# Infini-attention beside a 2-D Fourier filter on one core: causal zeros spread over three head steps, four copies from ScalarE to VectorE

## The chip, the core and the metric

The kernel runs on one core of a Trainium2 chip. The metric is device time in microseconds (us), here the median of several executions. The engines are TensorE (PE, with its weight loads as PEld), VectorE (DVE), ScalarE (ACT), GpSimd (POOL) and SyncE (SP), which only issues DMAs here. The engines work through their own instruction lists in program order and wait for one another on semaphores.

## What is computed

Two independent results stand side by side in the output. The first is an attention over 2048 positions with 32 heads of 18 columns, in four segments of 512: inside a segment a causal softmax, and beside it a linear memory that earlier segments have filled. A gate per head mixes both. The second is a filter in the frequency domain (a 2-D FFT, a product, the inverse).

```python
for s in range(N):                       # N = 4 segments of 512
    qs, ks, vs = q[:, :, s], k[:, :, s], v[:, :, s]
    logits = einsum("bhqd,bhkd->bhqk", qs, ks) * scale + mask   # causal
    a_dot = einsum("bhqk,bhkd->bhqd", softmax(logits), vs)
    pq = phi(qs)
    num = einsum("bhld,bhde->bhle", pq, M)
    den = einsum("bhld,bhd->bhl", pq, z)[..., None] + 1e-6
    o = g * (num / den) + (1.0 - g) * a_dot
    M = M + einsum("bhld,bhle->bhde", phi(ks), vs)
    z = z + einsum("bhld->bhd", phi(ks))
y = irfft2(rfft2(x) * W)                 # the second result
```

## The kernel before

The order of all instructions is written out by hand: Python generators are advanced one `yield` at a time, and what is emitted first stands first on its engine. The Fourier part and the projections come first, up to about 370 us. Then `attention` runs 133 head steps `t`. One step serves one head of 18 columns in one segment, and four steps make a quad `k` (32 quads: 4 segments of 8).

For each head, three things are done at different steps.

- **Maxima** (`s1`, lines 616 to 640), for the head of step `t+10`, so up to step 117. PE makes logits with queries on the partitions; VectorE takes their row maxima (L627, L633). At step `hh==1` of a quad, `mpath` (L641 to L656) brings the maxima of the quad two later into a bfloat16 pair `mh` on GpSimd (L648, L649); at `hh==3` PE transposes them (L652), ScalarE copies them (`mts`, L655), and GpSimd issues a DMA (L656) that lays them under the queries `Qs`, so that the next logits come out with the maximum subtracted.
- **Exponentials** (`s2`, L658 to L685), for the head of step `t`. PE makes the logits anew with keys on the partitions (L666, L670, L671, L675), ScalarE takes the exponential into three tiles of the quad: `P0` (key block 0 against 512 queries), `P1` (block 1 against 384 queries, then block 3 against 128) and `P2` (block 2 against 256). The first 128 columns of each block hold the diagonal, where the entries above it must become zero. `sel` does that for all four heads of a quad at once: on GpSimd by a selection (L679) in quads 0 to 28, on VectorE by a minimum with a tile `cap` (L680) in quads 29 to 31.
- **Products with the values** (`pv`, L686 to L697): for quad `k` in steps 4k+5 (`jj==0`, reads `P0`), 4k+6 (`jj==1`, reads the first 384 columns of `P1`) and 4k+7 (`jj==2`, reads the last 128 columns of `P1` and then `P2`). `pv_out` copies the sum to SBUF (L701).

In between, the background list `bg` advances at a rate of 1.2 pieces a step: `den`, `mixed`, `oproj`. `mixed(g)` interleaves `combine(g-1)` with `mem1(g,t)`. `combine` takes the attention output of a segment, multiplies it by the reciprocal of the softmax sum (a matmul that spreads the reciprocals over the partitions, L801, and VectorE's product, L806), adds the memory term (L807) and splits the sum into a high part (`oh`, ScalarE, L796) and a low part (`ol`, L797) for the output projection (L822). L797 and L807 are on GpSimd up to step 117, then on VectorE. `mem1` makes the memory term for five groups `t` of heads: a matmul `pn` (L764), a copy to `am` (L766), the spread reciprocals `pb` (L770) and the product (L771). The matmul outputs of all these pieces share one PSUM bank, tag `post`, so each of them waits until the piece before it has been read. `recip` prepares the reciprocals (DVE L720 and L721, ACT L723 and L724, POOL L725 to L727).

`later(k,f)` puts `f` on a list with the due step `now+k`. `due(t)` stands last in a step: it sets `now` to `t` and runs what is due. During step `t`, `now` is therefore still `t-1`.

```python
    def later(s,k,f): s.late.append((s.now+k,f))
    def due(s,now):
        s.now=now; L=s.late; s.late=[]
        for t,f in L:
            if t<=now: f()
            else: s.late.append((t,f))
```

Of the kernel before, what the change touches and what calls it, by code (L numbers as in the profile page):

```python
# [376 lines left out]
class ATT:  # L377
# [280 lines left out]
    def s2(s,t):  # L658
        nc=s.nc; k,hh=divmod(t,4); n,qd=divmod(k,2); h=4*qd+hh
        Q,K=s.Qs[n%3],s.Ks[n%4]; tp=s.tp  # L660
        if hh==0: s.P[k]=[tp.tile([128,4,w],F32,name=f"P{i}") for i,w in enumerate((512,512,256))]
        P=s.P[k]
        q=lambda o: Q[:110,h,o:]
        kk=lambda j: K[:110,h,128*j:128*j+128]
        p0=s.ps.tile([128,512],F32,name="s2",tag="s2")
        nc.tensor.matmul(p0,kk(0),q(0),start=True,stop=True)  # L666
        nc.scalar.activation(P[0][:,hh],p0,AF.Exp,scale=SC)  # L667
        yield
        p1=s.ps.tile([128,512],F32,name="s2",tag="s2")
        nc.tensor.matmul(p1[:,:384],kk(1),q(128),start=True,stop=True)  # L670
        nc.tensor.matmul(p1[:,384:],kk(3),q(384),start=True,stop=True)  # L671
        nc.scalar.activation(P[1][:,hh],p1,AF.Exp,scale=SC)  # L672
        yield
        p2=s.ps.tile([128,256],F32,name="s2",tag="s2")
        nc.tensor.matmul(p2,kk(2),q(256),start=True,stop=True)  # L675
        nc.scalar.activation(P[2][:,hh],p2,AF.Exp,scale=SC)  # L676
        if hh==3:
            def sel(x,pat):
                if k<29: nc.gpsimd.affine_select(out=x,in_=x,pattern=pat+[[1,128]],compare_op=OP.is_ge,fill=0.0,base=0,channel_multiplier=-1)  # L679
                else: nc.vector.tensor_tensor(x,x,s.cap[:,None,:].to_broadcast([128,4,128]),op=OP.min)  # L680
            sel(P[0][:,:,:128],[[0,4]])
            sel(P[1][:,:,:128],[[0,4]])
            sel(P[1][:,:,384:],[[0,4]])
            sel(P[2][:,:,:128],[[0,4]])
        yield  # L685
    def pv(s,k,jj):  # L686

# [73 lines left out]
    def mem1(s,g,t):  # L761
        nc=s.nc; r=126 if t<4 else 72
        pn=s.ps.tile([126,512],F32,name="pn",tag="post")
        nc.tensor.matmul(pn[:r],s.Mst[g][:r,t,:r],s.pq.pop((g,t))[:r],start=True,stop=True)  # L764
        am=s.tp.tile([126,512],F32,name="am",bufs=5)
        nc.scalar.copy(am[:r],pn[:r])  # L766
        if g<3: s.later(1,lambda: s.pq_load(g+1,t))
        yield
        pb=s.ps.tile([126,512],F32,name="pb",tag="post")
        nc.tensor.matmul(pb[:r],s.sel[:,t,:r],s.rc["rd"],start=True,stop=True)  # L770
        nc.vector.tensor_tensor(am[:r],am[:r],pb[:r],op=OP.mult)  # L771
        s.am[t]=am
        yield
# [319 lines left out]
```

## Time and profile before

| | |
|---|---|
| median of three executions | 743.37 us (743.27 to 746.62) |
| profiled execution | 743.75 us, its span 741.7 us |
| granted TensorE clock, mean | 0.993 |
| from the start of the head steps to the end of quad 28's zeros | about 370 to 668 us |
| VectorE minima of quads 29, 30, 31 | 676.15, 688.38 and 698.01 us, 2.49 us each for four |
| copies L766 | 15, 582 to 587 ns each on ScalarE |
| last instructions, output projection of segment 3 | 716 to 742 us |

The profile is one execution, recorded by the hardware. A timeline row has the start, the duration, the engine, the line of the kernel, the operation, output and inputs, and how many instructions were merged; in square brackets stands the idle time of the engine just before, and what ended it. Rows of four merged instructions show the time from the start of the first to the end of the last. On PE, matmuls overlap, so a row's duration is longer than the time until the next may start.

### The profile page before, as it was taken

To read this page: it belongs to the slowest core of one execution; us is meant where nothing else is said; L and a number is where in the kernel's file an instruction comes from. 1 tells how busy PE (TensorE), PEld (TensorE's weight loads), DVE (VectorE), ACT (ScalarE), POOL (GpSimd) and SP (SyncE) were. 2 spreads that over 40 slices of the span, in tenths; PEclk is the share of its full clock that TensorE was granted. 3 is DMA by queue.
4 is the path that set the end of the run, shared out by engine and by line. 5 is a ranking of instruction groups with operands and counts; after the bars stand their busy time and mean duration, and the time that the engine had idled before them with its cause. 6 is when DMAs were issued, how large, how long until landed. Compare 5 with 4: busy or idle time off the path is not lost.

```text
span 741.7 us, 14472 instructions
## 1 busy us (share of the span) xinstructions
PE 696.9 (94%) x5007; PEld 501.1 (68%) x5007; DVE 554.0 (75%) x1288; ACT 457.6 (62%) x1012; POOL 202.8 (27%) x401
## 2 busy tenths in 40 slices
PE   4998999999999999599999999999999999998897
PEld 4988779879789789499944444444565445663397
DVE  5999879899798788288587888887566875655533
ACT  3666796585694674144387777777566775656631
POOL 2111000100200114256155334545143762333010
PEclk9999999999999999899999999999999999999999
DMA  9884435555473368879637665777546765431052
GB/s 332 264 269 142 143 123 174 192 173 157 149 238 108 120 206 250 216 197 211 187 115 177 170 166 142 182 168 162 141 102 176 180 165 134 101 101 41 24 156 75
DMA packets 83245, 121.05 MB, mean 163 GB/s; under 512 B 11353, under 2 KB 50631, under 8 KB 83037
## 3 DMA queue, kind: packets, MB, share of 16 engines
q1 hardware_dynamic: 76580, 104.11, 49.5%
q0 software_dynamic: 6592, 16.03, 8.0%
q8 instruction: 39, 0.64, 0.4%
q14 instruction: 34, 0.27, 0.1%
HBM read 81.78 MB, written 38.24 MB: 162 GB/s over the span
## 4 chain that ended last, share of the span: by engine, by line
PE 72%; DMA 5%; DVE 4%; ACT 3%; issue 1%; POOL 1%; SPq 0%; DVEq 0%; ACTq 0%
PE pj L451 12%; PE pv L695 10%; PE s L623 9%; PE pjv L451 8%; PE po L822 6%; PE i L296 4%; PE i L307 4%; PE s L666 3%; PE s L670 3%; PE po L851 2%; PE pn L764 2%; DMA Ks<-qkD 2%; PE s L675 2%; PE s L632 2%; PE pm L508 2%
## 5 line engine op out<-in xcount | busy, mean ns | idle before, releaser
L627 DVE CUSTOM_DVE_ANT_0 junk<-s,mask 128x512 bf16<-128x512 f32 (+1 forms) x256 | 141.3, 552 | 61.1 <-PE s L623 57.6
L623 PE MATMUL s<-Ks,Qs 108*128 108x384 bf16 (+3 forms) x512 | 138.2, 302 | 9.9 <-DMA Ks<-qkD 7.3
L633 DVE TENSOR_REDUCE mx<-s 128x4 f32<-128x512 f32 x128 | 87.9, 687 | 20.2 <-PE s L632 18.4
L623 PEld LDWEIGHTS <-Qs 108*128 108x128 bf16 x512 | 50.6, 99 | 59.8 <-issue 44.4
L695 PE MATMUL pv<-P,vs 128*32 128x512 f32 (+3 forms) x1024 | 89.1, 442 | 1.1 <-ACT am L766 1.1
L679 POOL TENSOR_SCALAR_AFFINE_SELECT P<-P 128x512 f32<-128x512 f32 x116 | 70.1, 634 | 69.2 <-ACT P L667 61.4
L667 ACT ACTIVATE P<-s 128x512 f32<-128x512 f32 x128 | 76.4, 597 | 13.6 <-PE s L666 10.9
L676 ACT ACTIVATE P<-s 128x256 f32<-128x256 f32 x128 | 49.2, 385 | 51.3 <-PE s L675 50.8
L672 ACT ACTIVATE P<-s 128x512 f32<-128x512 f32 x128 | 76.2, 595 | 0.0
L451 PE MATMUL pj<-xh,wqkl 128*128 128x512 f32 x180 | 71.1, 395 | 0.0
L451 PE MATMUL pj<-xh,wqkh 128*128 128x512 f32 x180 | 71.1, 395 | 0.0
L451 PE MATMUL pj<-xl,wqkh 128*128 128x512 f32 x144 | 61.8, 429 | 0.0
L666 PE MATMUL s<-Qs,Ks 110*128 110x512 bf16 x128 | 48.8, 381 | 2.2 <-DMA Qs<-mts 1.4
L206 DVE TENSOR_TENSOR Z<-t,t 128x290 f32<-128x290 f32 (+1 forms) x96 | 48.4, 555 | 0.1
L451 PE MATMUL pjv<-wvh,xh 128*128 128x288 f32 x160 | 48.1, 303 | 0.0
L451 PE MATMUL pjv<-wvl,xh 128*128 128x288 f32 x160 | 46.2, 295 | 0.0
L206 DVE TENSOR_TENSOR t<-Z 128x580 f32<-128x580 f32 x64 | 46.1, 756 | 0.0
L498 POOL MEMSET vt<- 128x32 f32 x16 | 2.3, 161 | 150.4 <-PE pm L508 128.8
L632 PE MATMUL s<-tri,idb 128*128 128x128 bf16 x256 | 43.2, 220 | 0.0
L296 PE MATMUL i<-civ,Y 128*128 128x256 f32 (+1 forms) x288 | 40.2, 293 | 1.9 <-DVE t L206 1.7
L670 PE MATMUL s<-Qs,Ks 110*128 110x384 bf16 x128 | 41.9, 327 | 0.1
L142 PE MATMUL f<-ftab,eh 128*128 128x290 f32 (+1 forms) x160 | 30.7, 309 | 10.4 <-DMA ftab<-ftab 10.4
(169 smaller groups left out, 1628.6 us busy)
## 6 DMA issues: line engine op xcount, KB each, us to landing
qkD<-sp SPq DMA_DIRECT2D x36, 384.0 KB
Qs<-qkD SPq DMA_DIRECT2D x96, 144.0 KB
Ks<-qkD SPq DMA_DIRECT2D x96, 144.0 KB
xin<-xb SPq DMA_DIRECT2D x16, 384.0 KB
cfw<-cfw POOLq DMA_DIRECT2D x16, 384.0 KB, 4.5
civ<-civ POOLq DMA_DIRECT2D x16, 384.0 KB, 8.3
vs<-vD SPq DMA_DIRECT2D x16, 330.0 KB
vD<-vt SPq DMA_DIRECT2D x16, 311.0 KB
```

Source lines behind the costliest of these rows:

```text
L206: v.tensor_tensor(o,a,b,op=op)
L296: nc.tensor.matmul(p[:m,k],Y[i][:,q,c*128:c*128+m],cc[:,hl,o:o+256],start=n==0,stop=n==5)
L451: s.nc.tensor.matmul(out,a,b,start=i==0,stop=i==len(L)-1)
L623: nc.tensor.matmul(out,Q[:108,h,128*i:128*i+128],K[:108,h,:128*(i+1)],start=True,stop=True)
L627: nc.vector.tensor_tensor_reduce(out=junk[:,:w],in0=src,in1=s.mask[:,512-w:],scale=1.0,scalar=-3.0e38, op0=OP.add,op1=OP.max,accum_out=s.m ...
L633: nc.vector.tensor_reduce(out=s.mx[k][:,hh],in_=pa.rearrange("p (b c) -> p b c",c=128),axis=mybir.AxisListType.X,op=OP.max)
L666: nc.tensor.matmul(p0,kk(0),q(0),start=True,stop=True)
L667: nc.scalar.activation(P[0][:,hh],p0,AF.Exp,scale=SC)
L670: nc.tensor.matmul(p1[:,:384],kk(1),q(128),start=True,stop=True)
L672: nc.scalar.activation(P[1][:,hh],p1,AF.Exp,scale=SC)
L679: if k<29: nc.gpsimd.affine_select(out=x,in_=x,pattern=pat+[[1,128]],compare_op=OP.is_ge,fill=0.0,base=0,channel_multiplier=-1)
L695: nc.tensor.matmul(s.pvt[32*hh:32*hh+32,128*j:],vt[:,j,19*h:19*h+32],mv[0][:,hh,mv[1]],start=j==0,stop=j==2,skip_group_check=True)
```

## The change

The four selections of a quad are no longer emitted together in the last step of the quad. The one on `P0` stays. The one on the first 128 columns of `P1` is emitted at the end of the next step, those on `P2` and on the last 128 columns of `P1` at the end of the step after that, the one on `P2` first. This holds for GpSimd's selections and for VectorE's minima alike. The pattern of the selection, always the same, moves into `sel`.

The copy in `mem1` is emitted on VectorE instead of ScalarE when `now` is 119 or more: the last four of segment 3's five copies.

```diff
         if hh==3:
-            def sel(x,pat):
-                if k<29: nc.gpsimd.affine_select(out=x,in_=x,pattern=pat+[[1,128]],compare_op=OP.is_ge,fill=0.0,base=0,channel_multiplier=-1)
+            def sel(x):
+                if k<29: nc.gpsimd.affine_select(out=x,in_=x,pattern=[[0,4],[1,128]],compare_op=OP.is_ge,fill=0.0,base=0,channel_multiplier=-1)
                 else: nc.vector.tensor_tensor(x,x,s.cap[:,None,:].to_broadcast([128,4,128]),op=OP.min)
-            sel(P[0][:,:,:128],[[0,4]])
-            sel(P[1][:,:,:128],[[0,4]])
-            sel(P[1][:,:,384:],[[0,4]])
-            sel(P[2][:,:,:128],[[0,4]])
+            sel(P[0][:,:,:128])
+            s.later(2,lambda: sel(P[1][:,:,:128]))
+            s.later(3,lambda: sel(P[2][:,:,:128]))
+            s.later(3,lambda: sel(P[1][:,:,384:]))
```

```diff
         am=s.tp.tile([126,512],F32,name="am",bufs=5)
-        nc.scalar.copy(am[:r],pn[:r])
+        (nc.vector.tensor_copy if s.now>=119 else nc.scalar.copy)(am[:r],pn[:r])
```

## The prediction

> **What bounds the kernel now.** I read the page first, then the busy time by windows, the waits of PE, and the timelines of POOL, DVE, ACT and PE at every place where PE stood.
>
> ```profile
> span 741.7 us, 14472 instructions
> PE 696.9 (94%) x5007; PEld 501.1 (68%) x5007; DVE 554.0 (75%) x1288; ACT 457.6 (62%) x1012; POOL 202.8 (27%) x401
> ```
>
> ```profile
> 380.00:676.00 296.00, 290.14 (x2407) 152.09 (x2406) 214.30 (x630) 205.69 (x492) 132.92 (x240) 1.00 0.59 148
> ```
>
> (The last row is a window: its length, then the busy time of PE, PEld, DVE, ACT and POOL, the granted clock, the DMA share and GB/s.) TensorE bounds it. In the stage that the change touches first (quads 0 to 28, 380 to 676 us) PE is busy for 290.1 of 296.0 us, POOL for 132.9. The zeros are POOL's work there and hidden, as long as no PV matmul waits for them. So the first edit can only give back some of 5.9 us of PE's idle time, or take cover away. From quad 29 on (676 to about 704 us) the zeros are on DVE and PE has real holes; there the order on DVE and ACT counts.
>
> Each quad k has its exponentials in steps 4k to 4k+3 and its PV in three later steps: PV0 (reads P0) in 4k+5, PV1 (P1, first 384 columns) in 4k+6, PV2 (P1's last 128 columns first, then P2) in 4k+7.
>
> **The change part by part.**
>
> *Part 1, the zeros on POOL (quads 0 to 28).* No instruction is added or removed; `sel(P1[:128])` goes to the end of step 4k+4, P2 and P1's last columns to the end of 4k+5. `later(2)` and `later(3)` count from the step before, since `due` sets `now` last. The order of POOL becomes: P0, the DMA of the maxima (L656), first selection of P1, the two `mh` operations (L648, L649), P2, last selection of P1. What is queued in a step ahead of `due` (the pieces of `combine`, L797 and L807, and `recip`, L725 to L727) now stands ahead of zeros that used to be long done. On SP's queue nothing moves. PV1 waits for P1's first selection alone, PV2 for the last one.
>
> ```profile
> L679 POOL TENSOR_SCALAR_AFFINE_SELECT P<-P 128x512 f32<-128x512 f32 x116 | 70.1, 634 | 69.2 <-ACT P L667 61.4
> ```
>
> One selection takes 0.63 us; four in a row take 2.39 us (rows below), so they follow each other every 0.59 us. What it gives:
>
> ```profile
> 395.41 2.39 POOL L679 TENSOR_SCALAR_AFFINE_SELECT P<-P 128x512 f32<-128x512 f32 x4
> 397.75 0.61 POOL L656 DMA_DIRECT2D Qs<-mts  x1
> ```
>
> ```profile
> 394.42 0.24 ACT L655 COPY mts<-mt 32x128 bf16<-32x128 bf16 x1
> ```
>
> ```profile
> 404.13 0.39 PE L666 MATMUL s<-Qs,Ks 110*128 110x512 bf16 x1 [1.44 <-DMA Qs<-mts]
> ```
>
> The largest PE wait before 676 us: a logits matmul of quad 4 waits 1.44 us for the maxima's DMA, issued behind four selections at 397.75 though `mts` was ready at 394.66. Behind one selection it starts at about 396.0, 1.75 us earlier, more than the wait: **−1.44**, if the landing moves with the issue. Ahead of it one small loss eats into it:
>
> ```profile
> 391.37 0.22 POOL L649 TENSOR_TENSOR mh<-mg,mh 128x16 bf16<-128x16 f32 x1
> ```
>
> ```profile
> 392.66 0.86 PE L695 MATMUL pv<-P,vs 128*32 128x128 f32 x16
> ```
>
> Quad 1: the second `mh` lets POOL go at 391.55; P2 and the last P1 selection (0.59+0.63) end at 392.77, with a hand-over of some 0.05 us against PV2 at 392.66: +0.17. Net **−1.27**.
>
> What it costs elsewhere is read from the same sum, end of `mh` plus 1.22 us, against PV2. The first and the last of the usual quads:
>
> ```profile
> 382.29 0.22 POOL L649 TENSOR_TENSOR mh<-mg,mh 128x16 bf16<-128x16 f32 x1
> ...
> 663.59 0.22 POOL L649 TENSOR_TENSOR mh<-mg,mh 128x16 bf16<-128x16 f32 x1
> ```
>
> ```profile
> 384.42 0.86 PE L695 MATMUL pv<-P,vs 128*32 128x128 f32 x16
> ...
> 665.72 0.86 PE L695 MATMUL pv<-P,vs 128*32 128x128 f32 x16
> ```
>
> `mh` lets POOL go 0.17 us after its start, 382.46 and 663.76; 1.22 more gives 383.68 and 664.98, both 0.74 us ahead of PV2. Of the 29 quads taken in this way from the two timelines, 14 have 0.5 to 0.75 us to spare, 12 have more, quad 1 has none, and in two more `combine` puts operations in between:
>
> ```profile
> 581.19 0.22 POOL L649 TENSOR_TENSOR mh<-mg,mh 128x16 bf16<-128x16 f32 x1
> 581.36 1.27 POOL L797 TENSOR_TENSOR ol<-am,oh 126x512 fp32r<-126x512 f32 x1
> 582.60 1.27 POOL L807 TENSOR_TENSOR am<-ux,am 126x512 f32<-126x512 f32 x1
> ```
>
> ```profile
> 584.03 0.86 PE L695 MATMUL pv<-P,vs 128*32 128x128 f32 x16
> ```
>
> Quad 20: L797 and L807 were queued before `due`, so P2 starts at 583.84 and the last selection ends at 585.06. PV2 goes at 585.12 instead of 584.03: **+1.09**. Right behind it DVE waits for PE, too, so there is no backlog that would absorb the delay:
>
> ```profile
> 585.29 0.69 DVE L771 TENSOR_TENSOR am<-am,pb 126x512 f32<-126x512 f32 x1 [0.51 <-PE pb L770]
> ```
>
> Quad 28 has the same order:
>
> ```profile
> 669.03 2.52 POOL L807 TENSOR_TENSOR am<-ux,am 126x512 f32<-126x512 f32 x2
> 671.50 1.27 POOL L797 TENSOR_TENSOR ol<-am,oh 126x512 fp32r<-126x512 f32 x1
> 672.74 1.25 POOL L807 TENSOR_TENSOR am<-ux,am 126x512 f32<-126x512 f32 x1
> 674.21 0.22 POOL L649 TENSOR_TENSOR mh<-mg,mh 128x16 bf16<-128x16 f32 x1
> ```
>
> ```profile
> 669.23 0.68 DVE L806 TENSOR_TENSOR ux<-ux,pb 126x512 f32<-126x512 f32 x1
> ```
>
> ```profile
> 674.29 0.86 PE L695 MATMUL pv<-P,vs 128*32 128x128 f32 x16
> ```
>
> Quad 28: the second L807 needs the `ux` that DVE ends at 669.91, so it ends at about 671.2; P1's first selection makes 671.8; L797, L807 and both `mh` (674.21+0.17−671.50 = 2.88 us in the rows) make 674.65; P2 and the last selection 675.87. PV2 goes at 675.93: **+1.64**. Behind it on PE stand the `pb` of L770, L652 and the logits of step 120, and ACT's exponentials wait for these.
>
> *Part 2, the zeros of quads 29 to 31 and the four copies (L766) on DVE.* They move as before, P0 in step 4k+3; each copy leaves ACT's queue and enters DVE's. The largest hole:
>
> ```profile
> 676.15 2.49 DVE L680 TENSOR_TENSOR P<-P,cap 128x512 f32<-128x512 f32 x4
> 678.56 0.69 DVE L797 TENSOR_TENSOR ol<-am,oh 126x512 fp32r<-126x512 f32 x1
> 679.16 0.68 DVE L806 TENSOR_TENSOR ux<-ux,pb 126x512 f32<-126x512 f32 x1
> ```
>
> ```profile
> 677.79 0.60 ACT L796 CAST oh<-am 126x512 fp32r<-126x512 f32 x1
> ```
>
> ```profile
> 679.89 2.07 PE L764 MATMUL pn<-pq,Mst 126*126 126x512 f32 x2 [3.12 <-DVE ux L806]
> ```
>
> PE waits 3.12 us for `ux`, and four selections stand before it. With one, DVE would be free at 676.76; but L797 comes first and needs `oh`, which a closed row of ACT work delivers at 678.39. So the hole shrinks by **0.15** only; ACT is next in line. The copies cannot help, the first one moved comes behind this place.
>
> ```profile
> 688.95 0.59 ACT L766 COPY am<-pn 126x512 f32<-126x512 f32 x1 [1.27 <-PE pn L764]
> 689.43 0.39 ACT L676 ACTIVATE P<-s 128x256 f32<-128x256 f32 x1
> ```
>
> ```profile
> 690.86 0.38 PE L666 MATMUL s<-Qs,Ks 110*128 110x512 bf16 x1 [0.71 <-ACT P L667]
> ```
>
> The copy holds ACT for 0.48 us, ACT goes on without a gap until 690.8, and PE waits for it. Off ACT, the exponentials and PE come 0.4 us earlier. On DVE, idle there, the copy costs nothing that PE sees. Its price isn't shown: below, the 288-column copy (0.46, next row); above, 0.68 us for L771, which also reads PSUM over 512 columns. I take 0.60 to 0.69.
>
> ```profile
> L993 DVE COPY P<-po 128x288 f32<-128x288 f32 x4 | 1.8, 459 | 5.5 <-PE po L851 5.5
> ```
>
> ```profile
> 698.01 2.49 DVE L680 TENSOR_TENSOR P<-P,cap 128x512 f32<-128x512 f32 x4
> 700.42 0.94 DVE L721 RECIPROCAL ry<-ry 128x128 f32<-128x128 f32 x1
> 701.28 0.62 DVE L771 TENSOR_TENSOR am<-am,pb 72x512 f32<-72x512 f32 x1
> ```
>
> ```profile
> 701.96 0.93 PE L822 MATMUL po<-woh,oh 126*128 126x288 f32 x5 [0.94 <-DVE am L771]
> ```
>
> The end of the stage: L771 now stands behind P0, a copy, the reciprocal and one selection (0.60+0.60+0.86+0.60) instead of four selections and the reciprocal, and the row starts 0.45 earlier. L771 starts at 700.2 (697.56 and 2.66); PV1 (needs that selection) ends at 701.1, and the projection L822 starts there: **−0.85** in all for the copies and the order, the 0.4 included. From there to the end PE and the DMAs follow one another, so it stays.
>
> **Sum:** −1.27 +1.09 +1.64 −0.15 −0.85 = **+0.46 us**. The profiled execution took 743.75 us (span 741.7), 0.38 above the median of the runs, 743.37. Against the median: 743.8, say **743.9 us**.
>
> Bounds of the terms: DMA wait −1.44 to 0; quad 20 from +0.5 to +1.2 and quad 28 from 0 (if the pieces of `combine` come earlier) to +1.8; the tail −1.6 (both selections behind L771 and the copy gone from its way) to 0.
>
> **The clock** is one more term.
>
> ```profile
> 679.86:683.27 3.41, 3.38 (x9) 1.15 (x13) 0.69 (x1) 1.27 (x3) 0.00 (x0) 0.50 0.02 5
> ```
>
> This window's granted clock is 0.50: after the 3.12 us hole PE runs at half speed for 3.41 us, busy all the time, and 1.7 us are lost. The hole stays in my forecast (about 3.0 us, behind a new one of 1.6), so I keep the loss. The Trainium skill (TensorE: Matmul & The Clock Gate, What's actually happening) says that the clock halves after an idle window of about 3.4 us and that the windows run freely. [...] The trace agrees on the 3.41 us of the slow stretch, not on the whole idle window: the hole had 3.12 us. The first rival below is what this rule would do here.
>
> **Rivals.**
> - *The hole falls otherwise and the clock holds:* 1.7 us less, 742.2. For it: the hole gets shorter and starts at another moment. Against: it shrinks by 5% only. 0.20.
> - *The DMA doesn't land earlier:* the engines are 59% busy over the stage; if others hold the transfer, 1.27 comes back: 745.2. The row of all 32 speaks for it a little, the latencies lie far apart. 0.12.
>
> ```profile
> DMA to landing us min/median/max: 2.0/5.0/8.4
> ```
>
> The Trainium skill (DMA: Bandwidth & Descriptors, Anatomy of one DMA) gives 2.0 us plus bytes over 436e3 for such a DMA; an estimate from it, 2.02 us for 8 KB, would land at 399.8 and leave no wait to remove. Only the fastest one here agrees.
> - *Slower: PV2 waits in every usual quad.* The place is the last selection of P1 behind both `mh`. The point is the 0.74 us of the usual quad: if POOL is later by 1.0 us there (a `mh` that waits longer, a slower hand-over), 14 quads lose about 0.3 each, 4.2 us: 748.1. Against: the selections are all alike and `mh` keeps its place. 0.11.
> - *Faster, the change does what it seems meant to:* the two POOL waits don't show, DMA wait and copies pay in full, the clock holds: −1.44−0.15−0.85−1.7: 739.2. Against: the queued L797 and L807. 0.07.
>
> **How the numbers follow.** My forecast has 0.50. 0.5% is 3.7 us, about what a measurement of this kernel can tell from no change: within it lie the forecast, the first and the second rival, 0.82; slower 0.11, faster 0.07. The range leaves these two out and takes in 742.2 and 745.2 with the unknown terms, some 1.2 us on either side: 741.2 to 746.4; the forecast alone has 742.7 to 745.1.
>
> **What would show it.** The DMA wait at 404 us gone; new waits of PE for L679 near 584 (1.1 us) and 674 us (1.6 us), none in the usual quads; the hole before L764 still near 3 us, now behind `oh` of ACT; L766 on DVE 0.60 to 0.69 us; from quad 28's PV2 to the start of L822 26.7 us instead of 27.7 (701.96−674.29, less 0.15 and 0.85). Wrong if PE waits for L679 in many quads, if that hole closes, or if the clock column differs.

## The result and the profile after

The changed kernel takes 748.3 us (median of 21 executions, 745.4 to 756.5). The kernel before, executed beside it, takes 744.5 us (21 executions, 741.7 to 748.4). The ratio on record is 1.0062 (that of the two medians is 1.0052), with a 95% interval of 1.0043 to 1.0082: slower by 3.2 to 6.1 us, where the prediction had +0.5 us. The profiled execution took 747.5 us, near the median, against 743.75 us before. (The profile of experiment e5 below was of a disturbed execution and is not read.)

The page of the changed kernel, first the span and the busy times, then two groups (duration of all, mean of one in ns, idle time in front):

```profile
span 745.5 us, 14461 instructions
...
PE 698.6 (94%) x5007; PEld 504.0 (68%) x5007; DVE 556.1 (75%) x1292; ACT 455.5 (61%) x1008; POOL 204.9 (27%) x401
...
L695 PE MATMUL pv<-P,vs 128*32 128x512 f32 (+3 forms) x1024 | 89.7, 445 | 4.3 <-POOL P L679 2.6
...
L679 POOL TENSOR_SCALAR_AFFINE_SELECT P<-P 128x512 f32<-128x512 f32 x116 | 72.6, 639 | 35.7 <-ACT P L667 35.5
```

PE has hardly more to do, and of the 4.3 us that it waits ahead of value products (L695) 2.6 us are now due to the selections. The timeline of PE shows the places:

```profile
583.25 0.86 PE L695 MATMUL pv<-P,vs 128*32 128x128 f32 x16 [1.00 <-POOL P L679]
...
675.22 0.86 PE L695 MATMUL pv<-P,vs 128*32 128x128 f32 x16 [1.64 <-POOL P L679]
...
680.70 1.12 PE L764 MATMUL pn<-pq,Mst 126*126 126x512 f32 x2 [2.99 <-DVE ux L806]
...
710.13 0.38 PE L831 MATMUL pb<-rr,sel 96*126 96x512 bf16 x1
...
715.13 0.38 PE L831 MATMUL pb<-rr,sel 96*126 96x512 bf16 x1 [2.63 <-DVE ux L832]
```

The first three rows are what the prediction asked for: 1.0 us near 584, 1.6 us near 674, a hole of 3.0 us before L764; and the DMA wait at 404 us is gone. The fifth is not in it. L831 is the matmul that spreads the reciprocals for the last segment's five tiles. The second of them waits 2.63 us for PSUM that VectorE's product L832 has to read. The window after it (length, PE, PEld, DVE, ACT, POOL busy, granted clock, DMA share, GB/s) stands at half clock:

```profile
715.94:719.35 3.41, 3.41 (x16) 3.41 (x15) 2.61 (x4) 2.43 (x6) 0.00 (x0) 0.50 0.17 38
```

The same place in the kernel before, in the timelines of PE, SP, POOL and VectorE:

```profile
702.22 0.42 POOL L725 TENSOR_TENSOR ry<-ry,rw 128x128 f32<-128x128 f32 x1 [24.87 <-ACT rw L724]
```

```profile
705.43 0.32 SPq L733 DMA_DIRECT2D rr<-rrD  x1
...
708.93 1.34 SPq L784 DMA_DIRECT2D ux<-uD  x3
```

```profile
710.11 0.38 PE L831 MATMUL pb<-rr,sel 96*126 96x512 bf16 x1
...
712.89 0.38 PE L831 MATMUL pb<-rr,sel 96*126 96x512 bf16 x1 [0.41 <-DVE ux L832]
```

```profile
712.15 0.69 DVE L832 TENSOR_TENSOR ux<-ux,pb 126x512 f32<-126x512 f32 x1 [10.24 <-DMA ux<-uD]
```

And in the kernel after:

```profile
701.45 1.78 POOL L725 TENSOR_TENSOR ry<-ry,rw 128x128 f32<-128x128 f32 x1 [23.18 <-ACT rw L724]
```

```profile
701.66 1.28 DVE L680 TENSOR_TENSOR P<-P,cap 128x512 f32<-128x512 f32 x2
714.38 0.69 DVE L832 TENSOR_TENSOR ux<-ux,pb 126x512 f32<-126x512 f32 x1 [11.45 <-DMA ux<-uD]
```

```profile
706.29 0.32 SPq L733 DMA_DIRECT2D rr<-rrD  x1
...
709.70 1.28 SPq L784 DMA_DIRECT2D ux<-uD  x3
```

L725 belongs to the `recip` that makes the reciprocals `rr`; they go through memory, and L733 loads them. `ux` is the attention output, loaded back from memory (L784) for the product L832. Read from quad 28's PV2 on, which takes out what happened earlier (674.29 before, 675.22 after):

| from PV2 of quad 28, us | before | after | shift |
|---|---|---|---|
| projection L822 starts | 27.67 | 26.76 | −0.91 |
| L725 of POOL starts | 27.93 | 26.23 | −1.70 |
| L725 ends | 28.35 | 28.01 | −0.34 |
| ux loads issued (L784) | 34.64 | 34.48 | −0.16 |
| first L831 | 35.82 | 34.91 | −0.91 |
| first ux load used (L832) | 37.86 | 39.16 | +1.30 |
| second L831 | 38.60 | 39.91 | +1.31 |

PE arrives 0.91 us earlier; the prediction had 1.00 (0.15 and 0.85). The loads that it then needs are not earlier: the reciprocal started 1.70 us sooner, but its POOL operation L725, now beside two minima of quad 31 on VectorE, takes 1.78 us instead of 0.42, and SP issues the ux loads behind that chain in program order. The loads also take longer to land (39.16−34.48 = 4.68 us instead of 3.22). The hole grows by 0.91−0.16+1.46 = 2.21 us (2.63−0.41 = 2.22 in the rows), and half a clock over 3.41 us follows, an estimated 1.7 us at most. The third L831 stands 44.58 us behind PV2 instead of 41.74, so 2.84 of the 3.8 us that the span grew are lost here. Of the rest, 1.19 us came before the first PV2 (385.61 instead of 384.42 us), where PE waits for nothing that was changed, and −0.26 between the two PV2.

### The profile page after: what moved, and what is told of

It reads as the page before. It is cut to its first block, busy times and chain, and to the rows that moved or that the text cites. A ratio compares the mean times of both kernels' runs of the same rounds, so it can differ in the third digit from the quotient of the medians.

```text
span 745.5 us, 14461 instructions
## 1 busy us (share of the span) xinstructions
PE 698.6 (94%) x5007; PEld 504.0 (68%) x5007; DVE 556.1 (75%) x1292; ACT 455.5 (61%) x1008; POOL 204.9 (27%) x401
## 4 chain that ended last, share of the span: by engine, by line
PE 70%; DMA 6%; issue 4%; DVE 3%; ACT 2%; POOL 2%; SPq 1%; DVEq 0%; ACTq 0%; POOLq 0%
PE pj L451 11%; PE s L623 10%; PE pv L695 9%; PE pjv L451 8%; PE po L822 6%; PE i L307 4%; PE i L296 4%; PE s L666 3%; PE s L670 2%; PE po L851 2%; PE s L675 2%; PE s L632 2%; DMA Ks<-qkD 2%; PE pm L508 2%; PE pn L764 1%
## 5 line engine op out<-in xcount | busy, mean ns | idle before, releaser
L623 PE MATMUL s<-Ks,Qs 108*128 108x384 bf16 (+3 forms) x512 | 138.5, 303 | 11.7 <-DMA Ks<-qkD 9.8
L695 PE MATMUL pv<-P,vs 128*32 128x512 f32 (+3 forms) x1024 | 89.7, 445 | 4.3 <-POOL P L679 2.6
L623 PEld LDWEIGHTS <-Qs 108*128 108x128 bf16 x512 | 50.7, 99 | 61.3 <-issue 44.9
L679 POOL TENSOR_SCALAR_AFFINE_SELECT P<-P 128x512 f32<-128x512 f32 x116 | 72.6, 639 | 35.7 <-ACT P L667 35.5
```

The source lines that it names most:

```text
L623: nc.tensor.matmul(out,Q[:108,h,128*i:128*i+128],K[:108,h,:128*(i+1)],start=True,stop=True)
L679: if k<29: nc.gpsimd.affine_select(out=x,in_=x,pattern=[[0,4],[1,128]],compare_op=OP.is_ge,fill=0.0,base=0,channel_multiplier=-1)
L695: nc.tensor.matmul(s.pvt[32*hh:32*hh+32,128*j:],vt[:,j,19*h:19*h+32],mv[0][:,hh,mv[1]],start=j==0,stop=j==2,skip_group_check=True)
```

## Experiments

Theory T1: the loss beyond the prediction is this chain. Rivals: T2, the two waits of PV2 for POOL with what they set off; T3, chance in where PE's idle time falls; T4, the copies on VectorE. Each ratio is to the kernel before, executed on the same chip, with its 95% interval. Line numbers are those of the profile; edits keep them.

**e1, the copies alone.**

```diff
-        nc.scalar.copy(am[:r],pn[:r])
+        (nc.vector.tensor_copy if s.now>=119 else nc.scalar.copy)(am[:r],pn[:r])
```

> The kernel before with the four last copies of L766 on VectorE and nothing else. Theory T1 (the loss of the whole change sits after 704 us: the selections of quad 31 that now stand behind the reciprocal run beside L725 of POOL, SP's queue is held, the ux loads come late, and the hole before L831 halves the clock): the four selections still end ahead of the reciprocal, so L725 stays at 0.4 us, the hole before L831 stays at 0.4 us or below, and the time is 0 to 0.5 us less, ratio 0.999 to 1.000. Rival T4 (the copies on VectorE cost what was lost): ratio 1.004 to 1.006. Rival T3 (the loss is where the idle windows of PE fall by chance): any ratio of 0.997 to 1.003, with the granted clock as the only difference.

Measured: 1.0015 (0.999 to 1.0041), above the 0.999 to 1.000 that T1 expected. L725 takes 0.42 us and the hole before L831 0.61, as T1 says. But the last copy stands behind four minima on VectorE, and PE waits for it; the timeline of PE and the windows:

```profile
698.35 1.06 PE L695 MATMUL pv<-P,vs 128*32 128x512 f32 x8 [1.06 <-DVE P L680]
700.67 0.38 PE L770 MATMUL pb<-rd,sel 96*72 96x512 bf16 x1 [1.25 <-DVE am L766]
```

```profile
697.69:701.10 3.41, 1.50 (x13) 0.43 (x17) 3.41 (x6) 0.00 (x0) 0.00 (x0) 1.00 0.00 0
701.10:704.51 3.41, 3.41 (x17) 2.19 (x14) 0.92 (x2) 0.70 (x2) 1.14 (x3) 0.50 0.02 5
```

Two short holes fall into one stretch of 3.41 us, PE is busy for 1.50 us of it, and the next stretch runs at half clock. The copies are free only while the minima are dealt out. T4 as a cause of the whole loss falls.

**e2, the zeros on POOL alone.**

```diff
-            sel(P[0][:,:,:128])
-            s.later(2,lambda: sel(P[1][:,:,:128]))
+            df=s.later if k<29 else lambda i,f: f(); sel(P[0][:,:,:128])
+            df(2,lambda: sel(P[1][:,:,:128]))
...
```

> Only the zeros of POOL (quads 0 to 28) are dealt over three steps; those of VectorE stay together and the copies stay on ScalarE. T1: the waits for L679 near 584 (1.1 us) and 674 us (1.6 us) show, the DMA wait at 404 us is gone, L725 stays at 0.4 us, the hole before L831 near 0.4 us: +1.5 us in all, ratio 1.001 to 1.003. Rival T2 (the two waits of PV2 for POOL are what the whole change lost, by what they set off behind them): ratio 1.004 to 1.007.

Measured: 1.0037 (1.0015 to 1.0058), that is 1.1 to 4.3 us. Both waits are there, L725 takes 0.42 us, and the hole before L831 is small:

```profile
583.90 0.86 PE L695 MATMUL pv<-P,vs 128*32 128x128 f32 x16 [0.99 <-POOL P L679]
...
675.86 0.86 PE L695 MATMUL pv<-P,vs 128*32 128x128 f32 x16 [1.63 <-POOL P L679]
...
714.91 0.38 PE L831 MATMUL pb<-rr,sel 96*126 96x512 bf16 x1 [0.80 <-DVE ux L832]
```

Between the two theories: a good part of the loss, about half, sits here. It was in the prediction, as +1.46 us, and the interval holds that.

**e3, the zeros on VectorE alone** (`df=s.later if k>=29`, the copies on ScalarE).

> Only the zeros of VectorE (quads 29 to 31) are dealt over three steps; those of POOL stay together and the copies stay on ScalarE. T1: L725 of POOL runs beside two selections of quad 31 and takes over 1.2 us instead of 0.42, L733 and the ux loads are issued 0.6 to 0.9 us later, the hole before L831 is 2 us or more and half clock follows it: ratio 1.003 to 1.005. T2: nothing of the loss is here, ratio 0.998 to 1.000. T3: as T2, or the clock alone.

Measured: 1.0023 (0.9996 to 1.005), below the 1.003 to 1.005 that T1 expected, with an interval that holds both theories; the times alone do not decide. The profile does for the place of the hole, though the copies and POOL's selections are those of before:

```profile
700.18 2.04 POOL L725 TENSOR_TENSOR ry<-ry,rw 128x128 f32<-128x128 f32 x1 [22.93 <-ACT rw L724]
```

```profile
714.02 0.38 PE L831 MATMUL pb<-rr,sel 96*126 96x512 bf16 x1 [2.73 <-DVE ux L832]
```

**e4, the whole change with the loads early.** They read rows that earlier heads wrote.

```diff
             if t==125: lane.append(s.recip(s.rD[3],s.rrD[3],s.g1,False,"rr"))
+            if t==130: [s.ux_load(3,u) for u in range(3)]
...
-        for u in range(3): s.ux_load(3,u)
```

> The whole change, and the three first ux loads of the last group are issued at the start of step 130, ahead of L733 and of the transfers of U in SP's queue, instead of behind them. Their rows were written by earlier heads. T1: the loads land before 710 us, the hole before L831 (2.63 us in the profile of the changed kernel, 0.41 in that of before) and the half clock behind it go, though L725 is as slow as before: 3 to 4.5 us less than the changed kernel, ratio to the kernel before 0.999 to 1.002. T2 and T3: the ratio stays at 1.005 to 1.007.

Measured: 0.9989 (0.9961 to 1.0017). L725 is as slow as ever, but the loads no longer hang on it, and VectorE's product waits for PE instead of a DMA:

```profile
699.31 1.77 POOL L725 TENSOR_TENSOR ry<-ry,rw 128x128 f32<-128x128 f32 x1 [23.26 <-ACT rw L724]
```

```profile
708.61 0.69 DVE L832 TENSOR_TENSOR ux<-ux,pb 126x512 f32<-126x512 f32 x1 [7.82 <-PE pb L831]
```

PE has no wait of 0.4 us or more at L831, and no half clock there. The loss of the change is gone with an edit that touches none of its instructions.

**e5, the kernel before with the loads early** (the same edit).

> The kernel before with the three first ux loads of the last group at the start of step 130, as in e4. Theory T1 (the changed kernel loses its time because PE gets to the projection earlier while the chain reciprocal, SP's queue, ux loads is not earlier, and a hole and half clock follow): here the hole before L831 is only 0.4 to 0.8 us, so the early loads bring 0.4 to 0.8 us, ratio 0.999 to 1.000. Rival: the early loads are worth 4 us to any kernel (they also clear the DMA queue for what follows), ratio 0.994 to 0.996, and e4 then says nothing of what the change lost.

Measured: 0.9978 (0.9948 to 1.0008). More than expected, 1.6 us, with an interval that holds the expected 0.4 to 0.8 (the medians, 743.75 and 744.32 us, differ by 0.6). In the changed kernel the same edit is worth some 4.5 to 5.4 us (from 1.0050 in e11 or 1.0062 to 0.9989). About 3 to 4 us of what e4 gains are thus the change's own loss there, with some 2 us of uncertainty on each of the two.

**e6, quad 31's minima together again** (`df=s.later if k<31`, the rest as in the change).

> The whole change except for quad 31, whose four selections stay together in step 127, ahead of the reciprocal. T1: L725 of POOL is back at 0.42 us, the hole before L831 at 0.4 to 0.9 us without half clock behind it; the two waits for L679 (1.0 and 1.6 us) stay: ratio 1.001 to 1.003, 2 to 4 us less than the whole change. Rival T2 (the waits of PV2 for POOL and what they set off are the loss): ratio stays at 1.005 to 1.007.

Measured: 1.0029 (0.9998 to 1.0059). As T1 says, at the place in question:

```profile
703.14 0.42 POOL L725 TENSOR_TENSOR ry<-ry,rw 128x128 f32<-128x128 f32 x1 [24.90 <-ACT rw L724]
```

```profile
716.63 0.38 PE L831 MATMUL pb<-rr,sel 96*126 96x512 bf16 x1 [0.84 <-DVE ux L832]
```

But the half clock came elsewhere, as in e1, where PE waits for the last copy:

```profile
701.48 0.59 PE L770 MATMUL pb<-rd,sel 96*72 96x512 bf16 x1 [1.25 <-DVE am L766]
```

```profile
700.82:707.65 6.83, 6.17 (x32) 4.12 (x35) 2.01 (x4) 0.91 (x3) 1.14 (x3) 0.50 0.08 17
```

So e6 tells the cause of the hole, not its price.

**e7, the delay without the change.** The kernel before, with idle copies ahead of L725.

```diff
+        [nc.gpsimd.tensor_copy(w[:,2],y) for _ in range(4 if dst is s.rrD[3] else 0)]; nc.gpsimd.tensor_tensor(y,y,w[:,0],op=OP.subtract)
```

> The kernel before with four idle copies of 128x128 on POOL ahead of L725 in the recip of step 125 (about 1.4 us, what L725 was slowed by in the changed kernel); nothing else is touched and no selection is moved. T1: L729, L733 and the ux loads come 1.4 us later, the hole before L831 grows from 0.4 to 1.8 us (3 us if the loads also take 4.5 us instead of 3.3 to land); with half clock behind it the time is 3 to 4.5 us more, without it 1.4: ratio 1.002 to 1.006. Rival T3 (POOL's chain has slack there, the late loads were the DMA queue of that run): ratio 0.999 to 1.001.

Measured: 1.005 (1.0019 to 1.008), as large a loss as the whole change's, out of 1.4 us on a POOL that is otherwise idle:

```profile
700.44 1.36 POOL L725 CAST rw<-ry 128x128 bf16<-128x128 f32 x4 [25.52 <-ACT ry L723]
701.89 0.42 POOL L725 TENSOR_TENSOR ry<-ry,rw 128x128 f32<-128x128 f32 x1
```

```profile
713.74 0.58 PE L831 MATMUL pb<-rr,sel 96*126 96x512 bf16 x1 [2.69 <-DVE ux L832]
```

```profile
713.78:717.19 3.41, 3.41 (x14) 3.33 (x14) 3.38 (x5) 1.84 (x4) 0.00 (x0) 0.50 0.03 10
```

T3 falls: POOL's chain has no slack there, and its delay alone brings the hole and the half clock.

**e8, POOL's zeros in two steps** (with e4's loads).

```diff
-            s.later(3,lambda: sel(P[2][:,:,:128]))
-            s.later(3,lambda: sel(P[1][:,:,384:]))
+            s.later(c,lambda: sel(P[2][:,:,:128]))
+            s.later(c,lambda: sel(P[1][:,:,384:]))
```

Here `c` is 2 for quads 0 to 28 and 3 for the others.

> e4 (the whole change with the early ux loads), and on POOL (quads 0 to 28) both zeros of P1 and that of P2 are issued at the end of step 4k+4, so that they stand ahead of the mh operations and of the pieces of combine of step 4k+5. The waits of PE for L679 near 584 (1.0 us) and 674 us (1.6 us) go, the DMA of the maxima still stands behind one selection only: 2 to 3 us less than e4, ratio to the kernel before 0.995 to 0.997. If the waits are made up for later anyway (PE catches up on ACT or DMA), as e4: 0.998 to 1.000.

Measured: 0.9977 (0.9946 to 1.0008). No wait for L679 is left; a shorter one stands in its place (0.48 us, PE's transpose for `mh` of POOL at 675.5), and the profiled execution waits 1.87 us for a load of `Ks` at 486. The gain on e4, 0.9 us, is below the 2 to 3 expected and smaller than either interval.

**e9, a store held back** (the whole change; the first `ya` of segment 2's projection stands behind the ux loads on SP).

```diff
-                if hf==1: s.later(1,lambda tb=tb,ob=ob: ...
+                if hf==1: s.later(2 if g==2 and tb==0 else 1,lambda tb=tb,ob=ob: ...
```

> The whole change, with one store of the group before (ya of its first 128 rows, 288 KB) issued behind the three ux loads and the last transfer of U in SP's queue instead of between two transfers of U. If that store, which stands ahead of the ux loads in the DMA queues, is what makes them take 4.7 us instead of 3.2 to land: landing 3.2 us or less, hole before L831 1.0 us instead of 2.6, half clock gone there, 2 to 3 us less than the changed kernel, ratio 1.001 to 1.004. If the landing does not depend on it: hole 2.2 to 2.7 us, ratio 1.005 to 1.007.

Measured: 1.0003 (0.9975 to 1.0031), but the profiled execution is one of the longest of its twelve (749.6 us, their median is 745.6) and shows a landing of 4.92 us (711.55 to 716.47) and a hole of 2.09 us:

```profile
717.21 0.38 PE L831 MATMUL pb<-rr,sel 96*126 96x512 bf16 x1 [2.09 <-DVE ux L832]
```

The times speak for the store as a cause of the long landing, the profile against it. Inconclusive.

**e10, the recip operations on VectorE** (the whole change).

```diff
+        eg=nc.vector if dst is s.rrD[3] else nc.gpsimd; eg.tensor_tensor(y,y,w[:,0],op=OP.subtract)
+        eg.tensor_copy(w[:,1],y)
+        eg.tensor_tensor(w[:,2],y,w[:,1],op=OP.subtract)
```

> The whole change, with the three operations of the recip of step 125 (L725 to L727) on VectorE, where they stand ahead of the last two selections of quad 31, instead of on POOL beside them. Theory T1 (L725 was slowed by the selections that run beside it): the chain ends about 1.4 us earlier, L733 and the ux loads with it, hole before L831 1.2 us or less and no half clock behind it: 2.5 to 4 us less than the changed kernel, ratio 1.000 to 1.003. Rival (the three operations were not the late link; the landing of the loads or SP's queue is): hole 2 us or more, ratio 1.005 to 1.007.

Measured: 1.0004 (0.9981 to 1.0026). The order of the minima is that of the change, the meeting of the two engines is taken away (and L725 is shorter on VectorE, 0.28 us instead of 0.42):

```profile
701.33 0.28 DVE L725 TENSOR_TENSOR ry<-ry,rw 128x128 f32<-128x128 f32 x1
...
702.12 1.29 DVE L680 TENSOR_TENSOR P<-P,cap 128x512 f32<-128x512 f32 x2
```

```profile
712.63 0.38 PE L831 MATMUL pb<-rr,sel 96*126 96x512 bf16 x1 [0.45 <-DVE ux L832]
```

**e11, the change once more.**

> The whole change once more, unaltered, beside the others of this group: ratio 1.005 to 1.007, hole before L831 2.4 to 2.8 us with half clock behind it, waits for L679 of 1.0 and 1.6 us. Where the profile differs from the first one (the wait for Ks near 305 us, the start of the first PV2), it is what changes from one execution to the next. If chance decides (T3), the hole before L831 differs by 1 us or more.

Measured: 1.005 (1.0023 to 1.0077). The two waits are there again (0.99 and 1.63 us), L725 takes 1.77 us, half clock runs from 716.60 to 720.01 us, and

```profile
715.50 0.38 PE L831 MATMUL pb<-rr,sel 96*126 96x512 bf16 x1 [2.76 <-DVE ux L832]
```

What varies is PE's wait at about 310 us, ahead of L623 (7.28 us before and 9.80 in the first profile after, both for `Ks`; 7.82 here, where the profile shows no releaser); the first PV2 comes at 383.86 us here. The 1.19 us of the first profile were chance.

**e12, the low parts last** (e8, and from step 117 on L797 on VectorE behind the products).

```diff
-                eng().tensor_tensor(s.ol[u][:r],x[:r],s.oh[u][:r].bitcast(F32),op=OP.subtract)
+                low=lambda o=s.ol[u][:r],x=x[:r],h=s.oh[u][:r].bitcast(F32): eng().tensor_tensor(o,x,h,op=OP.subtract)
...
-                r=126 if t<4 else 72; x=xs[t]
+                r=126 if t<4 else 72; x=xs[t]; t>1 and s.now<117 and low()
...
-                    eng().tensor_tensor(s.am[t][:r],x[:r],s.am[t][:r],op=OP.add)
+                    eng().tensor_tensor(s.am[t][:r],x[:r],s.am[t][:r],op=OP.add); t>1 and s.now>=117 and low()
...
-            yield
+            t>4 and low(); yield
```

> e8 (zeros of POOL in two steps, copies and zeros of VectorE as in the whole change, early ux loads), and in combine from step 117 on the difference L797 is issued on VectorE behind the products of the same tile (L806, L807) instead of ahead of them, since it waits for oh of ScalarE. VectorE is free at about 676.8 us for L806, so the hole of 3.1 us before L764 falls to 1 us or less and the half clock behind it (1.7 us) goes: 3 to 4.5 us less than e8, ratio to the kernel before 0.992 to 0.995. If oh or the pb of PE is the next limit at once: hole stays over 2.5 us, ratio 0.997 to 0.999.

Measured: 0.9889 (0.9856 to 0.9922), 736.8 us, the fastest of all and faster than both kernels. The timelines of VectorE and PE:

```profile
675.47 0.69 DVE L680 TENSOR_TENSOR P<-P,cap 128x512 f32<-128x512 f32 x1
676.43 0.69 DVE L806 TENSOR_TENSOR ux<-ux,pb 126x512 f32<-126x512 f32 x1 [0.28 <-PE pb L801]
677.15 0.69 DVE L807 TENSOR_TENSOR am<-ux,am 126x512 f32<-126x512 f32 x1
678.28 0.69 DVE L797 TENSOR_TENSOR ol<-am,oh 126x512 fp32r<-126x512 f32 x1 [0.44 <-ACT oh L796]
```

```profile
677.17 1.12 PE L764 MATMUL pn<-pq,Mst 126*126 126x512 f32 x2 [0.67 <-DVE ux L806]
```

The hole before L764 falls to 0.67 us (3.12 in e8, 2.99 in the change), and the half clock behind it is gone.

**e13, the ry load behind the ux loads** (the whole change; L716 after L784 on SP).

```diff
-        b=s.recip(s.rD[3],s.rrD[0],s.g1,False,"rd"); next(b)
-        for u in range(3): s.ux_load(3,u)
+        b=s.recip(s.rD[3],s.rrD[0],s.g1,False,"rd")
+        for u in range(3): s.ux_load(3,u); next(b) if u==2 else None
```

> The whole change, with the ry load of the last group (L716, which waits on SP for rD and reads rows of 512 bytes) issued behind the three ux loads instead of ahead of them. The ux loads are issued 0.5 to 0.9 us earlier by that alone. If the ry load is what makes them land late: 3.2 us or less from issue to landing, hole before L831 under 0.6 us, no half clock, ratio 1.000 to 1.003. If not: 4.4 us or more from issue to landing, hole 1.7 to 2.2 us, ratio 1.003 to 1.006.

Measured: 1.0036 (1.0009 to 1.0062). The loads still take 4.64 us (709.80 to 714.44); the `ry` load is not what holds them. The hole of 1.76 us brings no half clock:

```profile
715.18 0.38 PE L831 MATMUL pb<-rr,sel 96*126 96x512 bf16 x1 [1.76 <-DVE ux L832]
```

```profile
713.41:716.82 3.41, 1.65 (x13) 1.61 (x12) 2.31 (x4) 0.92 (x2) 0.00 (x0) 1.00 0.42 144
716.82:720.23 3.41, 3.41 (x27) 3.38 (x26) 3.28 (x6) 1.97 (x6) 0.74 (x1) 1.00 0.34 90
```

**e14, e12 without the change:** the kernel before with the edits of e4 and e12.

> e12 without any of the change: the kernel before, with the early ux loads and with L797 behind the products. If the zeros dealt out on VectorE are what lets L806 go early, the four selections still stand before it here, the hole before L764 is 2.4 us or more with half clock behind it: ratio 0.994 to 0.998, 4 us or more above e12. If the order of L797 alone closes the hole: as e12, 0.987 to 0.991.

Measured: 0.9944 (0.9921 to 0.9967). Four minima stand before L806, and the hole before L764 is back:

```profile
679.52 2.02 PE L764 MATMUL pn<-pq,Mst 126*126 126x512 f32 x2 [2.52 <-DVE ux L806]
```

Against e12 this is some 4 us, with about 3 us of uncertainty either way. e14 leaves out the whole change, POOL's part too: in the two profiles 1.9 us of the difference lie between the first PV2 and quad 28's, where chance moves about as much, and 3.5 us behind it (62.4 us to the end of the span in e12, 65.9 here). So with L797 out of the way and the loads early, the dealt minima and the copies on VectorE are worth about 3.5 us in this pair; in the change as it was made, neither was so.

## Why the prediction was wrong

It was wrong in one step, which it put in one sentence: "From there to the end PE and the DMAs follow one another, so it stays." The other terms came out close to what was worked out, the first with some luck:

| term | predicted, us | shown |
|---|---|---|
| DMA wait at 404 us goes | −1.44 | gone in every profile with dealt zeros on POOL; in those without, 1.44, 0.51, 0.54 and 1.05, and none at that place in e3: the forecast took the largest of five |
| quad 1's PV2 comes late | +0.17 | 2.27 us behind PV1 instead of 2.11: +0.16 |
| quad 20's PV2 waits for L679 | +1.09 | wait 1.00, PV2 4.13 us behind PV1 instead of 3.06: +1.07 |
| quad 28's PV2 waits for L679 | +1.64 | wait 1.64 |
| hole before L764 shrinks | −0.15 | 3.12 to 2.99 |
| copies and order up to L822 | −0.85, with the −0.15 PV2 to L822 26.7 | 26.76, shift −0.91 |
| copy on VectorE | 0.60 to 0.69 us each | 0.68 to 0.69 |
| from there to the end | 0 | third L831 at +2.84 instead of −1.00 (−0.15 and −0.85): 3.8 us |

*POOL's part.* Over the stretch from the first quad's PV2 to quad 28's, the five profiles with the selections together (before, e1, e3, e7, e14) have 287.6 to 290.0 us, mean 289.1; the eight with three steps (after, e2, e4, e6, e9, e10, e11, e13) have 289.6 to 291.9, mean 290.8. The difference, 1.7 us, stands beside −1.27+1.09+1.64 = 1.46; single pairs scatter (before and after alone give −0.26). With the 2.84 us of the end it makes 4.5 us, inside the measured 3.2 to 6.1. The two with two steps (e8, e12) have 289.3 and 288.1. No usual quad waits: the slower rival did not occur, and the second one neither (the DMA did land earlier). The wait that the forecast calls the largest before 676 us is so only from 380 us on; at 310 us PE waits 7.28.

*The end.* What it missed has two halves. The −0.15 and −0.85 move PE alone. PE then meets loads which hang on another chain (reciprocal, ScalarE, POOL's L725 to L727, a round trip through memory, SP's list) and were already late by 0.41 us before. And that chain could not move with PE, because the same dealing put two minima beside L725. The prediction named L725 to L727 only among what stands ahead of selections on POOL; beside VectorE's zeros it gave them no price. It also said that on SP's queue nothing moves, which holds for the order and misses what the order does: the ux loads, which need nothing of this chain, stand behind it. e10 takes away the meeting, e4 the hanging together, e7 puts the delay alone into the kernel before; all three came out as T1 expected, e4 at the edge of its range. e4 and e10 keep both waits of PV2 for POOL, so T2 does not explain the rest of the loss.

The Trainium skill (SBUF — State Buffer, SBUF: two separate sides) says that a GpSimd operation and a VectorE operation with two inputs in SBUF exclude each other through one pair of ports, whole instruction by whole instruction. L725 beside the minima, 1.78 us instead of 0.42, agrees: it ends 0.29 us after the second minimum. The kernel before already shows this price, in the last `recip`, where L833 has both inputs in SBUF:

```profile
717.17 0.69 DVE L833 TENSOR_TENSOR ux<-ux,am 126x512 f32<-126x512 f32 x1
```

```profile
717.20 0.95 POOL L725 TENSOR_TENSOR ry<-ry,rw 128x128 f32<-128x128 f32 x1 [13.70 <-ACT rw L724]
```

L725 starts 0.03 us behind L833, takes 0.95 us and again ends 0.29 us after it. That such a meeting has a price could have been read from these rows before the prediction. That whichever starts first keeps the ports is seen in e4: L725 starts at 714.55 and takes 0.43 us, and L833, from 714.70, takes 0.82 instead of 0.69. It is not seen beside the minima, where L725's record starts 0.21 us ahead of them, in e3 0.47 us, and L725 waits all the same; why stays open.

*The clock.* The prediction kept one half clock, behind the hole before L764. It is there (681.81 to 685.22). A second one comes behind the new hole. Rival one, that the clock holds, did not occur.

*Open.* Of the hole's 2.2 us, 1.46 are the longer landing of the ux loads (4.4 to 4.9 us in the profiles of after, e3, e7, e9, e11 and e13; 2.9 to 3.6 in those of before, e1, e2, e6 and e10; in e2 and e6 at most, since L832 waits for PE there). The `ry` load is not its cause (e13); e9 does not settle the store; other causes were not tried. The longer landing came with the delay alone in e7 (4.51 us). It is not more data: in the 6 us from the issue of the loads the queues move 1.15 MB before and 1.14 after, but in the first 3 us the DMA engines are 85% busy before and 66% after.

## What to carry to other kernels

When an edit brings PE earlier to a place, follow each operand it reads next back to its own chain, and ask of every engine on that chain what the same edit has put beside it; a gain that reaches one operand only becomes a hole. Look in an in-order DMA queue for loads that wait behind a chain they don't need: issuing three of them earlier was worth 4.5 to 5.4 us in the changed kernel, about as much as the change had lost, and some 1.6 us or less without the change. And a change that pays nothing may be waiting for the next obstacle: the dealt minima and the copies were worth about 3.5 us in one pair of profiles once L797 no longer stood in front of L806 and the loads came early.

## What the hardware showed beside this

The granted clock goes by stretches of 3.41 us whose borders do not follow the holes: in the profile after, half clock starts at 302.93, 681.81, 715.94 and 743.25 us, each a whole number of such stretches from the others. PE need not be idle for a whole stretch to get half clock in the next: 1.50 us busy of 3.41 (e1, two holes of about 1 us) gave it, and so did 1.72 us (e13, 675.86 to 679.28) and 1.76 us (e6, 697.41 to 700.82). 1.65 us (e13, a hole of 1.76) did not. So the busy time that the trace shows does not decide alone, and what else counts is open. The Trainium skill (TensorE: Matmul & The Clock Gate, What's actually happening) has the length and the free running, and the trace agrees; its whole idle window is not needed here. In the kernel before, the hole of 3.12 us lay almost wholly within one stretch, and one stretch of half clock followed. In e1 a hole of the same length lay across a border, 1.98 us of it ahead, and two stretches ran at half clock (677.2 to 684.0). So the same hole can cost, as an estimate, up to 1.7 us more in one execution than in another.
